# The first MLP's last 768 tokens by the seven-product 2x2 scheme that its second MLP already uses

## Chip, cores and metric

One core of one Trainium2 chip runs the kernel. The metric is device time in microseconds (us), the median of several executions; lower is better. TensorE (PE) multiplies, VectorE (DVE), ScalarE (ACT) and GpSimd (POOL) work element by element, SyncE (SP) issues nearly all DMA transfers.

## The reference

Attention over a window of 64 tokens on q, k, v of 4 x 8 x 576 x 64 gives `x`, 2304 tokens of 512 channels. Then come two MLPs, with the matrices `w_in` 512x2048, `w_out` 2048x512 in the first and `w_gate`, `w_val` 512x1536, `w_out` 1536x512 in the second:

```
h = x @ w_in
g = np.maximum(h, 0.0) + np.log1p(np.exp(-np.abs(h)))
x = g @ w_out
gate = 1.0 / (1.0 + np.exp(-(x @ w_gate)))
val = x @ w_val
return (gate * val @ w_out)
```

## The kernel before

Each float32 operand is kept as two fp32r tiles, a high part and the remainder, and each product is three matmuls into one accumulator (`mm3`, lines 393 to 396: high x high, high x low, low x high). All three lines appear with the same counts in the trace.

The first MLP goes block by block over the tokens (`BLOCKS1`, 512, 384, 384, 512 and 512). For each of 16 feature chunks f of 128, `m1_proj` (line 415) makes 12 matmuls into a bank `h0` or `h1`, ACT takes softplus in the bank (`m1_act`, 421) and writes the high part (`g_hi`, 426), DVE the low one (`g_lo`, 433), and two chunks later `m1_out` (438) makes 12 matmuls into four accumulator banks `acc0` to `acc3`. At a block's end `m1_copy` (450) drains them through a ring of three `stage` tiles (`STB`), and `m1_send` (458) stores them to the DRAM tensor `x2d`. The attention is done in 36 groups of 64 tokens: eight ahead of the first block, the others scattered between the blocks' matmuls. Groups of blocks 0 and 1 turn their probabilities on PE (`att_transpose`, 333), later ones with DVE and a trip through DRAM (`att_blocks`, `att_send`, `att_fetch`).

The second MLP (`m2_prod` 500, `m2_after` 532, `m2_out` 557) already uses a 2x2 block scheme: 768 tokens are two halves of 384, a quad is one 2x2 block of `w_gate` and `w_val`, and seven products M0 to M6 of combined weights and combined inputs stand for eight. The combined weights of a quad, 1.79 MB, are made during the first MLP (`c_sums` 193, `c_sum4` 204, `c_hi`, `c_lo`), stored to DRAM by `c_send`, and loaded by `wc_load` (237) through the two-buffer ring `xt`, which the first MLP's inputs use before. The inputs come back from `x2d` by `x2_load`, are combined by `x2_sum` and split by `x2_hi` and `x2_lo` (468 to 489).

The order of every engine's work is written into the program. Up to the first `m2_prod`, `lead_in` (944) places the operations of all engines by a model of their costs (`traits`, 786) and due times, keeping PE's sequence of `slots`; from there on the order is that of slots and offsets as written. Engines run their own queue in order and wait for each other by semaphores.

Of the kernel before, what the change touches and what calls it, by code (L numbers as in the profile page):

```python
# [41 lines left out]
def tile_kernel(ctx: ExitStack, tc: tile.TileContext, qk, vt, w1, w2, wg, wv, wo, out):  # L42
# [70 lines left out]
    place = list(range(NSLOT)) + [None] * len(seq2) + list(range(NSLOT - NF2, NSLOT))  # L113
# [77 lines left out]
    sum_t, send_t = {}, {}  # L191

    def c_sums(f):
        i = len(seq1) + 2 * f
# [6 lines left out]
        sum_t[f] = x  # L201

    def c_sum4(f):
        g = bits_t[len(seq1) + 2 * f].bitcast(F32)[:, 0]
        nc.vector.tensor_tensor(out=g[:, HC:], in0=g[:, HC:], in1=sum_t[f][:, HC:], op=ALU.subtract)

    def c_part(f, part):
        i = len(seq1) + 2 * f
        b = bits_t[i].bitcast(F32)
        if part in "av":  # L210
            k = "av".index(part)
            o = raw_t[i][:, k].bitcast(F32R).rearrange("p (e n) -> p e n", e=2)
            return b[:, k], o, 2 * k * DM
        if f not in send_t:
            send_t[f] = main.tile([P, 2, 2 * DM], U32, tag="raw", name="sumr", bufs=RB).bitcast(F32R)
        o = send_t[f]
        if part == "x":
            return sum_t[f], o[:, 0].rearrange("p (e n) -> p e n", e=2), 4 * DM
# [858 lines left out]
```

## Time and profile before

| | us |
|---|---|
| median of 3 runs (range) | 894.87 (894.35 to 895.14) |
| the profiled execution | 894.63 |
| its span in the trace | 892.8 |
| PE busy in the span | 884.1 (99%) |
| DVE, ACT, POOL busy | 523.7, 399.6, 153.7 |
| DMA queues busy, mean of 16 engines | 55.9% of the span, 177.59 MB |

The span runs from the first to the last instruction; the execution takes 1.8 us more around it. A matmul's row shows its own latency; because they are pipelined, the distance between starts is what one costs. The granted clock of PE is shown as a share of full speed.

### The profile page before, as it was taken

How to read it: one execution, taken by the hardware profiler on the slowest of the kernel's cores; microseconds unless marked ns; L12 is line 12 of the kernel's file. 1: busy time of each engine (PE TensorE's matmuls, PEld its weight loads, DVE VectorE, ACT ScalarE, POOL GpSimd, SP SyncE). 2: the span in 40 equal slices, each digit the busy share in tenths (PEclk: the TensorE clock that was granted, in tenths of full speed). 3: DMA queues.
4: the chain of work that ended last, by engine and by line, in shares of the span. 5: the costliest groups of instructions: out<-in, count | busy, mean ns of one | idle time of the engine just before them, and what ended most of it. 6: DMA issues, size and time to landing. Idle time of an engine off the chain costs nothing.

```text
span 892.8 us, 13509 instructions
## 1 busy us (share of the span) xinstructions
PE 884.1 (99%) x5033; PEld 796.5 (89%) x5035; DVE 523.7 (59%) x921; ACT 399.6 (45%) x892; POOL 153.7 (17%) x157
## 2 busy tenths in 40 slices
PE   9999999999999999999999999999999999999998
PEld 7688789999999888888889999999999999999997
DVE  5898876556555656365515667668445447444444
ACT  6867857546764755345323333334222225222222
POOL 4001102102110220002001333331111112111110
PEclk9999999999999999999999999999999999999999
DMA  9946346766786775683306565545454445544441
GB/s 348 395 158 207 134 163 211 248 198 229 265 270 208 239 235 163 212 284 130 130 1 255 221 256 201 206 176 216 178 212 156 161 163 208 185 165 165 165 166 72
DMA packets 56211, 177.59 MB, mean 199 GB/s; under 512 B 6096, under 2 KB 21456, under 8 KB 51536
## 3 DMA queue, kind: packets, MB, share of 16 engines
q1 hardware_dynamic: 56000, 176.58, 55.9%
q8 instruction: 40, 0.66, 0.3%
q14 instruction: 27, 0.22, 0.1%
q10 hardware_dynamic: 144, 0.13, 0.0%
HBM read 139.72 MB, written 36.96 MB: 198 GB/s over the span
## 4 chain that ended last, share of the span: by engine, by line
PE 98%; ACT 1%; DVE 1%; POOL 0%; issue 0%; POOLq 0%
PE h L394 17%; PE h L396 17%; PE h L395 17%; PE acc L394 11%; PE acc L395 11%; PE acc L396 11%; PE at L289 3%; PE at L376 2%; PE at L396 2%; PE at L395 2%; PE at L394 2%; PE acc L289 1%; PE h L406 1%; PE acc L338 0%; ACT w L179 0%; POOL w L330 0%
## 5 line engine op out<-in xcount | busy, mean ns | idle before, releaser
L512 DVE TENSOR_TENSOR w<-h,w 128x384 f32<-128x384 f32 x216 | 117.1, 556 | 159.5 <-PE h L396 156.8
L394 PE MATMUL h<-w,wc 128*128 128x384 f32 x504 | 169.0, 335 | 0.1
L396 PE MATMUL h<-w,wc 128*128 128x384 f32 x504 | 168.9, 335 | 0.0
L395 PE MATMUL h<-w,wc 128*128 128x384 f32 x504 | 168.7, 335 | 0.0
L524 POOL TENSOR_TENSOR g<-w,g 128x384 fp32r<-128x384 f32 x70 | 73.9, 1056 | 296.7 <-ACT g L517 252.1
L394 PE MATMUL h<-xt,w 128*128 128x512 f32 (+1 forms) x320 | 119.4, 373 | 0.6 <-ACT w L179 0.5
L394 PE MATMUL acc<-g,w 128*128 128x512 f32 (+1 forms) x320 | 119.5, 374 | 0.0
L396 PE MATMUL h<-xt,w 128*128 128x512 f32 (+1 forms) x320 | 117.9, 368 | 1.0 <-DVE w L187 1.0
L396 PE MATMUL acc<-g,w 128*128 128x512 f32 (+1 forms) x320 | 117.7, 368 | 0.0
L395 PE MATMUL acc<-g,w 128*128 128x512 f32 (+1 forms) x320 | 117.6, 368 | 0.0
L395 PE MATMUL h<-xt,w 128*128 128x512 f32 (+1 forms) x320 | 117.6, 368 | 0.0
L436 DVE TENSOR_TENSOR g<-h,g 128x512 fp32r<-128x512 f32 (+1 forms) x80 | 50.7, 634 | 82.9 <-ACT g L430 82.6
L394 PEld LDWEIGHTS h<-w,wc 128*128 128x128 f32 x504 | 94.6, 188 | 2.3 <-DVE w L512 0.4
L395 PEld LDWEIGHTS h<-w,wc 128*128 128x128 f32 x504 | 94.6, 188 | 2.0
L396 PEld LDWEIGHTS h<-w,wc 128*128 128x128 f32 x504 | 94.6, 188 | 0.0
L423 ACT ACTIVATE h<-h 128x512 f32<-128x512 f32 (+1 forms) x80 | 43.2, 540 | 106.6 <-PE h L396 104.4
L517 ACT CAST g<-w 128x384 fp32r<-128x384 f32 x72 | 36.9, 513 | 118.5 <-DVE w L512 118.5
L396 PEld LDWEIGHTS h<-xt,w 128*128 128x128 f32 x320 | 60.0, 188 | 9.5 <-DVE w L187 2.0
L394 PEld LDWEIGHTS h<-xt,w 128*128 128x128 f32 x320 | 60.1, 188 | 9.0 <-ACT w L179 0.6
L394 PEld LDWEIGHTS acc<-g,w 128*128 128x128 f32 x320 | 60.1, 188 | 8.0
L396 PEld LDWEIGHTS acc<-g,w 128*128 128x128 f32 x320 | 60.1, 188 | 7.7
L330 POOL TENSOR_TENSOR p<-p,st 128x512 f32<-128x512 f32 (+1 forms) x28 | 27.8, 996 | 226.8 <-DVE st L325 151.4
(129 smaller groups left out, 1438.5 us busy)
## 6 DMA issues: line engine op xcount, KB each, us to landing
wc<-wcd SPq DMA_DIRECT2D x36, 1792.0 KB, 7.2
qk<-in_qk SPq DMA_DIRECT2D x28, 512.0 KB, 4.8
wcd<-raw SPq DMA_DIRECT2D x24, 512.0 KB, 3.3
w<-in_w SPq DMA_DIRECT2D x16, 512.0 KB, 9.4
raw<-in_w SPq DMA_DIRECT2D x16, 512.0 KB, 4.6
v<-in_vt SPq DMA_DIRECT2D x25, 256.0 KB, 3.7
raw<-in_wg SPq DMA_DIRECT2D x12, 512.0 KB, 4.7
raw<-in_wv SPq DMA_DIRECT2D x12, 512.0 KB, 6.1
```

Source lines behind the costliest of these rows:

```text
L289: nc.tensor.matmul(out=s[:, j, :w], lhsT=t[:, 0, j, :], rhs=t[:, 1, j, :w], start=g >= NG0, stop=g >= NG0 or j == NPAIR - 1)
L330: nc.gpsimd.tensor_tensor(out=p[:, :, :w], in0=p[:, :, :w], in1=st[:, 2, :].unsqueeze(2).to_broadcast([P, NPAIR, w]), op=ALU.mult)
L376: nc.tensor.matmul(out=o[h * Q:(h + 1) * Q, j, :], lhsT=v[:w, (2 * j + h) * Q:(2 * j + h + 1) * Q], rhs=pt[:w, h, j], start=True, stop=True)
L394: nc.tensor.matmul(out=o, lhsT=lh, rhs=rh, start=first, stop=False)
L395: nc.tensor.matmul(out=o, lhsT=lh, rhs=rl, start=False, stop=False)
L396: nc.tensor.matmul(out=o, lhsT=ll, rhs=rh, start=False, stop=last)
L406: nc.tensor.matmul(out=idle["out"], lhsT=t[:, 0, :P], rhs=t[:, 1], start=True, stop=True)
L423: nc.scalar.activation(out=t, in_=t, func=AF.Softplus)
L436: nc.vector.tensor_tensor(out=g[:, 1, :n], in0=t, in1=g[:, 0, :n].bitcast(F32), op=ALU.subtract)
L512: nc.vector.tensor_tensor(out=out, in0=a, in1=b, op=op)
L517: nc.scalar.copy(out=g[:, 0, :HALF], in_=t)
L524: eng.tensor_tensor(out=g[:, 1, :HALF], in0=t, in1=g[:, 0, :HALF].bitcast(F32), op=ALU.subtract)
```

## The change

The first MLP's last 768 tokens leave the block loop; three blocks of 512 remain (`BLOCKS1`). The 768 tokens become one pass of eight quads (`NS1` = 1): a quad is a 2x2 block of `w_in`, two chunks of 128 features each way. Seven products of six matmuls of 384 columns (`s_prod`) are combined by ACT and DVE (`s_copy`, `s_mix`) into four feature-by-token parts; each gets softplus, high and low part (`s_act`, `s_hi`, `s_lo`), and then `s_out` multiplies three chunks of 128 tokens of each part with the features' 128 `w_out` rows, 512 wide, as the moving operand, into six accumulators laid token by channel. At the end `s_drain` turns each accumulator in 32x32 squares on DVE and `s_send` stores it to `x2d` by four DMAs in pieces of 32 floats.

The combined weights of these quads are rebuilt from the split weights in SBUF (`c_join` adds high and low) and take the same way through DRAM; those of the second MLP follow later (`COMBO1`, `COMBO2`: start and distance in us). The attention output of these 12 groups goes to DRAM (`att_out`, `att_put`, tensor `x1d`) and comes back by `x2_load`. The four first feature chunks of block 1 are done in two halves of 256 tokens (`SPLIT`). Attention is placed by times (`NEXT`, `REST`), all of it before the new stage. The planner now covers the new stage too, some of its constants change, and temporary tiles of the second MLP lie in other slots, five halves in place of six. In the second MLP's first quad PE's order is M0 M1 o0 o1 M2 M3 o2 M4 M5 o3 o4 M6 o5, as before, o0 to o5 being the last six `s_out`. The core of the diff:

```
-BLOCKS1 = [512, 384, 384, 512, 512]
+BLOCKS1, NS1, SPLIT = [512, 512, 512], 1, 4
...
+DENSE, NEXT, REST = (6.9, 11.0, 9.6), (62.8, 97.8), (120.5, 273.9)
+COMBO1, COMBO2, WOF, WOG, XT = (143.2, 12.7), (248.7, 17.4), 9.0, 12.0, 33.9
+URGE, FAR_MARGIN, X_MARGIN, HURRY = 10, 0.8, 2.0, 1.5
...
+    x1d = dram.tile([KC, P, NT - NT1], F32, tag="x1d", name="x1d")
     x2d = dram.tile([KC, P, NT], F32, tag="x2d", name="x2d")
-    wcd = [dram.tile([P, 14 * HC], F32, tag=f"wcd{f}", name=f"wcd{f}") for f in range(NF2)]
+    wcd = [dram.tile([P, 14 * HC], F32, tag=f"wcd{q}", name=f"wcd{q}") for q in range(NQ)]
...
+    def c_join(q, k):
+        if q not in join_t:
+            join_t[q] = main.tile([P, 2, DM], U32, tag="bits", name="bits", bufs=1)
+        w = w_t["w1", 2 * q + k].bitcast(F32)
+        nc.vector.tensor_tensor(out=c_bits(q)[:, k], in0=w[:, 0], in1=w[:, 1], op=ALU.add)
...
+    UNITS = []
+    for b, n in enumerate(BLOCKS1):
+        if b == 1 and SPLIT:
+            UNITS += [(b, 0, n // 2, 0, SPLIT), (b, n // 2, n, 0, SPLIT), (b, 0, n, SPLIT, NF1)]
+        else:
+            UNITS.append((b, 0, n, 0, NF1))
...
+    def att_out(g, engine):
+        x = main.tile([P, 512], F32, tag="stage", name="xo", bufs=STB)[:, :NPAIR * Q]
+        x_t[g] = x.rearrange("p (j n) -> p j n", j=NPAIR)
+        (nc.scalar.copy if engine == "act" else nc.vector.tensor_copy)(out=x_t[g], in_=o_t.pop(g))
+
+    def att_put(g):
+        t0 = g * Q - NT1
+        nc.sync.dma_start(out=x1d[:, :, t0:t0 + Q].rearrange("k p n -> p k n"), in_=x_t.pop(g))
+
+
     def mm3(o, lh, ll, rh, rl, first, last):
...
     def m1_proj(b, f):
-        n = BLOCKS1[b]
-        h = psum(f"h{f % 2}")[:, :n]
-        proj(h, w_t["w1", f], xt_t[b], n)
+        block, cols, n = cols_of(b)
+        h = psum(bank1[b, f])[:, :n]
+        proj(h, w_t["w1", f], xt_t[block][:, :, :, cols], n)
...
     def m1_out(b, f):
-        n = BLOCKS1[b]
+        block, cols, n = cols_of(b)
...
-        if f == 0:
-            acc_t[b] = [psum(f"acc{c}")[:, :n] for c in range(KC)]
+        if block not in acc_t:
+            acc_t[block] = [psum(f"acc{c}")[:, :BLOCKS1[block]] for c in range(KC)]
         for c in range(KC):
-            mm3(acc_t[b][c], w[:, 0, c * P:(c + 1) * P], w[:, 1, c * P:(c + 1) * P], g[:, 0, :n], g[:, 1, :n],
-                f == 0, f == NF1 - 1)
...
+            mm3(acc_t[block][c][:, cols], w[:, 0, c * P:(c + 1) * P], w[:, 1, c * P:(c + 1) * P], g[:, 0, :n], g[:, 1, :n],
+                f == 0 and not cols.start, f == NF1 - 1)
...
-        t0 = (2 * s + col) * HALF
-        nc.sync.dma_start(out=t, in_=x2d[2 * row:2 * row + 2, :, t0:t0 + HALF].rearrange("k p n -> p k n"))
+        src, t0 = (x1d, (2 * s + col) * HALF) if s < NS1 else (x2d, (2 * (s - NS1) + col) * HALF)
+        nc.sync.dma_start(out=t, in_=src[2 * row:2 * row + 2, :, t0:t0 + HALF].rearrange("k p n -> p k n"))
...
     def x2_hi(s, k, kc):
-        c = pair(2 * k, 1 + s, F32R, 2, DM)[:, kc, :, :HALF]
+        slot = index["w1", 2 * k + kc + 2]
+        c = pair(slot, 0, F32R, 2, DM)[:, slot % 2, :, :HALF]
...
+    AFTER = (2, 4, 5, 6)
+
+    def quad(j):
+        return half(0, (4, 3, 2, 4)[j])
+
+    def s_prod(s, f, k):
+        o = h_t[s, f, k] = psum(f"h{(7 * (s * NQ1 + f) + k) % 2}")[:, :HALF]
+        product(o, s, f, k)
+
+    def s_copy(s, f):
+        nc.scalar.copy(out=half(0, 0), in_=h_t.pop((s, f, 0)))
+
+    def s_mix(s, f, k):
+        m1, u2, lo, hi, sa = (half(0, i) for i in range(5))
+        o = h_t.pop((s, f, k))
+        if k == 1:
+            tt(u2, o, m1, ALU.add)
+        elif k == 2:
+            tt(sa, o, m1, ALU.add)
+        elif k == 3:
+            tt(lo, o, u2, ALU.add)
+        elif k == 4:
+            tt(hi, o, lo, ALU.add)
+            tt(u2, o, u2, ALU.add)
+        elif k == 5:
+            tt(lo, lo, o, ALU.subtract)
+        else:
+            tt(sa, o, u2, ALU.add)
+
+    def s_act(s, f, j):
+        nc.scalar.activation(out=quad(j), in_=quad(j), func=AF.Softplus)
+
+    def s_hi(s, f, j):
+        g = g_t[s, f, j] = main.tile([P, 2, NMAX], F32R, tag="g", name="g1", bufs=GB)
+        nc.scalar.copy(out=g[:, 0, :HALF], in_=quad(j))
+
+    def s_lo(s, f, j, engine):
+        g = g_t[s, f, j]
+        eng = nc.gpsimd if engine == "pool" else nc.vector
+        eng.tensor_tensor(out=g[:, 1, :HALF], in0=quad(j), in1=g[:, 0, :HALF].bitcast(F32), op=ALU.subtract)
+
+    def token_acc(s, c):
+        if (s, c) not in acc_t:
+            acc_t[s, c] = psum(f"acc{c}") if c < KC else psum("at", 2)
+        return acc_t[s, c]
+
+    def s_out(s, f, j, c):
+        g, w = g_t[s, f, j], w_t["w2", 2 * f + j % 3 % 2 + (j == 2)]
+        cols = slice(c * P % HALF, c * P % HALF + P)
+        mm3(token_acc(s, c), g[:, 0, cols], g[:, 1, cols], w[:, 0, :], w[:, 1, :], f == 0 and j < 2,
+            f == NQ1 - 1 and j > 1)
+
+    def s_drain(s, c):
+        x = x_t[s, "y", c] = main.tile([P, 512], F32, tag="stage", name="x2", bufs=STB)
+        nc.vector.transpose(out=x, in_=acc_t[s, c])
+
+    def s_send(s, c):
+        x, t0 = x_t.pop((s, "y", c)), NT1 + 2 * s * HALF + c * P
+        o = x2d[:, :, t0:t0 + P].rearrange("c (b x) n -> x (c b) n", x=32)
+        for a in range(4):
+            nc.sync.dma_start(out=o[:, :, 32 * a:32 * (a + 1)],
...
+    for c in range(NS1 * NQ1):
+        s, f = divmod(c, NQ1)
+        prods = [(s_prod, s, f, k) for k in range(7)]
+        late_q = [(s_out, s, f, j, 3 * j + i) for j in range(2) for i in range(3)]
+        outs = tail
+        for entry in "M0 M1 o0 o1 o2 M2 M3 o3 o4 o5 M4 M5 a0 a1 a2 M6 a3 a4 a5".split():
+            kind, k = {"M": prods, "o": outs, "a": late_q}[entry[0]], int(entry[1])
+            if k < len(kind):
+                slots.append(kind[k])
+        tail = [(s_out, s, f, j, (0, 3)[j - 2] + i) for j in (2, 3) for i in range(3)]
...
+        elif fn is s_out and f == NQ1 - 1 and rest[0] > 1:
+            c = rest[1]
+            at(i + 1, -50, s_drain, b, c)
+            at(i + 1, -49, s_send, b, c)
...
+    n1 = BLOCKS1[1] // Q // 2
+    for p in range(n1):
+        for k in range(2):
+            attention(NG0 + 2 * p + k, NEXT[0] + p * (NEXT[1] - NEXT[0]) / max(n1 - 1, 1), False)
+    nf = (NT // Q - NG0) // 2 - n1
+    for p in range(nf):
+        for k in range(2):
+            attention(NG0 + 2 * (n1 + p) + k, REST[0] + p * (REST[1] - REST[0]) / (nf - 1), False)
...
+    timely(when[s0] - XT, -1, swap_pools, 0)
+    for k, name in enumerate(NAMES):
+        timely(when[s0] - XT, k, x2_load, 0, name)
```

A seam is named below by its two sides: the one into the new stage follows the last block, the one out of it leads into the second MLP.

## Rows read from the trace of the kernel before

**Rows 1.** The page's first part: span, and busy time of each engine.

```profile
span 892.8 us, 13509 instructions
PE 884.1 (99%) x5033; PEld 796.5 (89%) x5035; DVE 523.7 (59%) x921; ACT 399.6 (45%) x892; POOL 153.7 (17%) x157
```

**Rows 2.** Busy time by stretch: PE, PEld, DVE, ACT, POOL, PEclk, DMA share, GB/s.

```profile
30.00:129.00 99.00, 97.47 (x544) 80.00 (x545) 87.15 (x126) 71.28 (x130) 5.69 (x6) 1.00 0.58 206
129.00:470.00 341.00, 341.00 (x2049) 306.70 (x2048) 188.12 (x340) 185.35 (x433) 46.34 (x43) 1.00 0.60 199
470.00:887.00 417.00, 416.93 (x2182) 388.62 (x2181) 229.12 (x411) 119.83 (x239) 90.10 (x83) 1.00 0.50 185
```

**Rows 3.** Timeline of PE, first block: first and last of 72 matmuls in a row.

```profile
60.19 0.39 PE L394 MATMUL h<-xt,w 128*128 128x512 f32 x1
...
76.28 0.39 PE L396 MATMUL acc<-g,w 128*128 128x512 f32 x1
```

**Rows 4.** Timeline of PE, second MLP: first and last of 21 matmuls in a row.

```profile
483.04 0.33 PE L394 MATMUL h<-w,wc 128*128 128x384 f32 x1
...
486.51 0.34 PE L396 MATMUL h<-w,wc 128*128 128x384 f32 x1
```

**Rows 5.** Groups by line and shape: count, busy us, mean ns, idle before.

```profile
L394 PE MATMUL h<-xt,w 128*128 128x512 f32 x192 | 75.9, 395 | 0.6 <-ACT w L179 0.5
...
L394 PEld LDWEIGHTS h<-xt,w 128*128 128x128 f32 x320 | 60.1, 188 | 9.0 <-ACT w L179 0.6 <-issue 0.6
...
L394 PE MATMUL h<-xt,w 128*128 128x384 f32 x128 | 43.5, 340 | 0.0
```

**Rows 6.** Timeline of PE around one attention group's transposes: start, duration in us.

```profile
108.30 0.60 PE L338 MATMUL at<-ident,p 128*128 128x128 f32 x4
108.66 0.48 PE L394 MATMUL h<-xt,w 128*128 128x512 f32 x1
108.97 0.40 PE L395 MATMUL h<-xt,w 128*128 128x512 f32 x1
```

**Rows 7.** Timeline of PE, first block, the longest hole after the start.

```profile
92.87 0.40 PE L395 MATMUL h<-xt,w 128*128 128x512 f32 x1
94.23 0.50 PE L396 MATMUL h<-xt,w 128*128 128x512 f32 x1 [0.96 <-DVE w L187]
```

**Rows 8.** Timeline of ACT: the exponentials of two attention groups, from table to table.

```profile
147.61 1.28 ACT L316 ACT_TABLE_LOAD   x1
...
153.71 0.47 ACT L423 ACTIVATE h<-h 128x384 f32<-128x384 f32 x1
```

**Rows 9.** Busy time by stretch, twenty us of the first block, columns as in Rows 2.

```profile
40.00:60.00 20.00, 20.00 (x90) 16.55 (x89) 19.03 (x27) 11.76 (x16) 0.00 (x0) 1.00 0.60 206
```

**Rows 10.** Groups by line and shape, columns as in Rows 5: DVE, POOL and ACT.

```profile
L512 DVE TENSOR_TENSOR w<-h,w 128x384 f32<-128x384 f32 x216 | 117.1, 556 | 159.5 <-PE h L396 156.8 <-issue 1.3 <-ACT w L533 1.2
...
L524 POOL TENSOR_TENSOR g<-w,g 128x384 fp32r<-128x384 f32 x70 | 73.9, 1056 | 296.7 <-ACT g L517 252.1 <-issue 42.8 <-PE h L396 1.9
...
L423 ACT ACTIVATE h<-h 128x384 f32<-128x384 f32 x32 | 15.2, 475 | 36.0 <-PE h L396 33.9 <-DVE bits L168 2.0
...
L228 POOL TENSOR_TENSOR raw<-bits,raw 128x512 fp32r<-128x512 f32 x7 | 9.1, 1295 | 57.2 <-ACT raw L223 57.2
```

**Rows 11.** DMA issues: count, KB each, median us from issue to landing.

```profile
wc<-wcd SPq DMA_DIRECT2D x36, 1792.0 KB, 7.2
...
pt<-pd SPq DMA_DIRECT2D x84, 64.0 KB, 3.1
...
x2d<-x SPq DMA_DIRECT2D x12, 256.0 KB, 2.1
```

**Rows 12.** Timeline at the seam into the second MLP: ACT, then PE.

```profile
479.01 0.59 ACT L454 COPY x<-acc 128x512 f32<-128x512 f32 x1 [1.60 <-DMA x2d<-x]
...
481.99 0.34 PE L396 MATMUL h<-w,wc 128*128 128x384 f32 x1
482.40 0.44 PE L394 MATMUL h<-w,wc 128*128 128x384 f32 x1
```

More of the change, by code (lines that the diff above doesn't have):

```diff
@@ L75, in tile_kernel @@
     NS2 = NT // (2 * HALF)
+    NSL = NS1 + NS2 - 1
+    NT1 = sum(BLOCKS1)
+    NQ1 = NF1 // 2
+    NQ = NQ1 + NF2
     NCH = 2 * HALF // P
@@ L112, in tile_kernel @@
     WO_AT = len(seq1) + len(seq2)
[L113 removed]
+    index = {key: i for i, (key, _) in enumerate(allw)}
+    place = list(range(NSLOT)) + [None] * len(seq2) + [index["w2", f] for f in range(NF2)]
     pair_t, raw_t, bits_t, w_t = {}, {}, {}, {}
@@ L200, in c_sums @@
         nc.vector.tensor_tensor(out=a21, in0=a11, in1=a21, op=ALU.subtract)
[L201 to L218, printed above, removed]
-        return b[:, 0, HC:], o[:, 1, :DM].rearrange("p (e n) -> p e n", e=2), 6 * DM
@@ new lines, in c_sum4, with c_part @@
+    def c_sum4(q):
+        g = c_bits(q)[:, 0]
+        nc.vector.tensor_tensor(out=g[:, HC:], in0=g[:, HC:], in1=sum_t[q][:, HC:], op=ALU.subtract)
+    def c_part(q, part):
+        if q < NQ1 and part == "a":
+            w = w_t["w1", 2 * q]
+            return None, w.rearrange("p e n -> p (e n)"), 0
+        if part == "s4":
+            if q not in send_t:
+                send_t[q] = main.tile([P, 512], F32R, tag="stage", name="sumr", bufs=STB)
+            return c_bits(q)[:, 0, HC:], send_t[q], 6 * DM
+        i = len(seq1) + 2 * (q - NQ1) if q >= NQ1 else ("c", q)
+        if i not in raw_t:
+            raw_t[i] = main.tile([P, 2, 2 * DM], U32, tag="raw", name="raw", bufs=RB)
+        k = int(part == "v")
+        t = sum_t[q] if part == "x" else c_bits(q)[:, k]
+        return t, raw_t[i][:, k].bitcast(F32R), "avx".index(part) * 2 * DM
@@ new lines, in tile_kernel, with attention, put @@
+    timed = {}
+    def attention(g, t, near):
+        odd = g % 2
+        if near:
+            def put(off, order, fn, *args):
+                at(t + off, order, fn, *args)
+        else:
+            def put(off, order, fn, *args):
+                timed[fn, *args] = t + 2.9 * off + order / 400
+        far = grp_block[g][0] >= FAR
+        put(0, 20, att_scores, g)
+        put(1, -30, att_max, g)
+        put(2, -30, att_exp, g)
+        put(4 - near, -33, att_sum, g)
+        put(4 - near, -32, att_norm, g)
@@ new lines, in traits @@
+        if fn is s_hi:
+            f, j = rest
+            return "act", 0.42, [(s_act, a, f, j)], [("g", GB, (s_out, a, f, j, 2 if j % 2 == 0 else 5))]
+        if fn is s_lo:
+            return THIRDS, 0, [(s_hi, a, *rest)], []
+        if fn is s_out:
+            f, j, c = rest
+            deps = [(s_lo, a, f, j), (*slots[pos[fn, a, *rest] - 1], None)]
+            if f == 0 and j < 2 and a == 0:
+                deps += [(m1_copy, NB1 - 1, k) for k in range(KC)] + [(att_out, g) for g in grp_block if g * Q >= NT1]
+            elif f == 0 and j < 2:
+                deps += [(s_drain, a - 1, c)]
+            return "pe", 0.68, deps, []
```

448 lines of the change are left out of this document (271 added, 177 removed).

## The prediction, made before the change was run

> **What bounds the kernel now.** I read the page's first part, then busy time by stretch, then the timeline of PE. PE is busy for 884.1 of 892.8 us [rows 1]. By stretch, PE is never idle from 129 to 470 us, and for 0.07 us from 470 to 887 [rows 2]; the first block's 99 us hold 1.53 us of idle time, most of it one hole in which PE waited for the low part of a weight: 1.36 us between starts where 0.23 is normal [rows 7]. So the time is the sum of what PE has to stream, at a granted clock of 1.00 (2.4 GHz). DVE is busy for 88% of the first block and 55% of the stretch to 470 us [rows 2]. Even at 19.03 of 20 us DVE held nothing up [rows 9]: a busy neighbour costs nothing here until one of its results comes late.
>
> **What one matmul costs.** From the first to the last of 72 matmuls of 512 columns are 71 distances in 16.09 us, 0.2266 us each [rows 3]; at 384 columns 20 distances take 3.47 us, 0.1735 us each [rows 4]. The line through both gives 0.1204 us at 256 columns.
>
> **PE, removed and added.** Rows 5 show one of six such lines each: the first MLP has 6 x 192 = 1152 matmuls of 512 columns and 6 x 128 = 768 of 384, so 261.0 + 133.2 = 394.3 us. Afterwards: blocks 0 and 2 have 768 matmuls of 512; block 1 has 12 x 24 = 288 of 512 and, in its split chunks, 2 x 4 x 24 = 192 of 256; the eight quads have 8 x 7 x 6 = 336 of 384 and 8 x 12 x 3 = 288 of 512. That is 1344 x 0.2266 + 336 x 0.1735 + 192 x 0.1204 = 304.6 + 58.3 + 23.1 = 386.0 us. The gain is **8.3 us**, small because only the projection loses a product in eight (48 matmuls, 8.3 us). The output products keep their columns; 512 in place of 384 wide saves 1.3 us of fixed cost and the split gives that back.
>
> The 256-column price is not in the trace. Its bounds are 0.107 (the columns alone at 2.4 GHz) and 0.1735 (the 384 row): -2.6 to +10.2 us over 192. A weight load lasts 188 ns [rows 5], but 384 columns already pass every 173 ns, so loads overlap; I take the line. The Trainium skill ("TensorE: Matmul & The Clock Gate", section "LDWEIGHTS (loading the stationary operand)") gives columns / 1.2 ns, 107 ns for 128. By that the load just fits under 120 ns; were the 188 ns row the pace, the sum would be 13 us worse. No run here shows 256 columns.
>
> **Attention on PE.** Eight groups in place of six turn on PE, since block 1 now has 512 tokens. One group's four transposes take 0.36 us and the next matmul 0.08 us more [rows 6]: **+0.9 us** for two. Scores and values stay 28 groups after the opening.
>
> **The first block and the split.** The first block carries up to four pairs of groups where it had three, beside a DVE at 88% [rows 2]. Bounds: the present hole goes (-1.1 us) or two like it come (+2.3); I take 0, as DVE at 95% held nothing up [rows 9]. In the split a step of PE is 12 x 0.12 = 1.44 us. A bank is wanted again one projection and two outputs later, 4.3 us, of which softplus, high and low part need some 1.2 us (475 ns for ACT's step at 384 [rows 10], less at 256). A pair's exponentials keep ACT from softplus for 6.1 us [rows 8]. One pair (`REST`, 137.5 + 6 us) falls there: 0 to 3 us, I take **+0.8**.
>
> **The new stage.** A quad is 42 x 0.1735 + 36 x 0.2266 = 15.4 us of PE. DVE mixes seven times, 3.9 us at 0.556; four low parts take 0.556 each on DVE or 1.056 on POOL [rows 10]. The eight extra weight sets cost DVE some 5 us each (two joins, three sums, a difference and three low parts, these on POOL at up to 1.295 [rows 10]). From 129 to 470 us DVE rises from 188 to some 188 + 31 + 18 + 40 - 17 (the blocks' low parts) = 260 us, 78%. Slack: a product's bank is wanted 3.1 us later, after one product and three outputs; its mix needs 0.6. The tightest wait is the second feature part: from M4 to its first output PE has M5, three outputs and M6, 4.1 us, against two mixes, two ACT steps of 0.48 and POOL's 1.06, some 3.2 with hand-overs. Cover of about 1 us: 0 to 8 us lost, I take **+0.5**, since the second MLP runs the same way with still less slack between products without a hole [rows 2].
>
> **Moved work.** The second MLP's sets are made later; inputs are copied, stored, reloaded, combined and split ahead of the stage, and again for the second MLP during it. All of this is ACT, DVE, POOL and DMA work with tens of us of lead: nothing on PE. Cover gone, a late set would cost one 7.2 us load [rows 11]. DMA gains 8 x 2 x 1.79 MB beside 177.6 and some 3 MB for the inputs, a share of 60% growing to about 70% [rows 2]. SP gets about 90 more issues and loses eight; new waits on it (inputs stored before they are reloaded, combined weights before their load) stand ahead of loads that are due later. I cost them at nothing, up to 2 us.
>
> **The seam out of the new stage.** Six DVE drains replace nothing the block loop had there except four copies, now earlier. Counting from the second MLP's M0, outputs end at 2.8, 3.4, 6.2, 8.9, 9.6 and 11.3 us. Only three stage tiles exist, so drains 3 to 5 wait for stores 0 to 2, and DVE, in order, then holds back the mixing of M4 to M6 behind them, for which PE waits as soon as its two banks are full. Before, such a wait (1.60 us, on ACT) let PE lose 0.24 us [rows 12]. A store is 256 KB in pieces of 128 bytes, not in the trace. Bounds: 2.1 us, like the same bytes in long rows; 12.4 us, four times the 3.1 us of a 64 KB fetch in 512-byte pieces [rows 11]. I take 3.3, nearer to the same bytes, since consecutive issues overlap. One after another from 3.6 us, the third then ends at 13.5, 2.1 after its drain could start; less 1 us of slack of the banks: **+1.1 us**. Below nothing it cannot go.
>
> **Sum.** 894.6 - 8.3 + 0.9 + 0.8 + 0.5 + 1.1 = 889.6 us against the profiled execution (span 892.8 and 1.8 around it); the median shown is 0.24 higher: **889.8 us**.
>
> **Rivals.** *Late stores at the seam (slower).* With T us per store PE loses 3.6 + 3T - 11.4 - 1.0 us. At T = 5.0 the rest of the gain is gone, from 5.6 the kernel is slower by 0.2%, at the upper end, 12.4, the time is about 917. For it: short pieces, a load of 1.79 MB just ahead of them in the queue, in-order DVE. Against: the copies before lost 0.24 us in the same place. The Trainium skill ("DMA: Bandwidth & Descriptors", Specifications) wants 512 bytes or more per piece for full rate and says that below it the engine reads before it writes. That rule speaks for this rival; if each store took twice the 3.3 us, 11.0 us would be lost and the time 899.7. Chance 0.12.
>
> *The chain within a quad takes the gain.* If DVE, with weight sets in front of the mixes, misses the second part's deadline by 1 us in each quad, 8 us go: 897.3. Against: rows 9. Chance 0.13, half of it with only a part lost, near 894.
>
> *256 columns do not come faster than 384.* 10.2 us back: 900.0. Against: loads overlap. Chance 0.07.
>
> **How the numbers follow.** The forecast has 0.68, with its own range 886.5 to 893: no new stall gives 887.4, the bounds of the split, first block and stage the rest. A measurement tells about 0.2% (1.8 us) from no change, so faster means below 893.1 and slower above 896.7. The forecast's mass and a sliver of the chain make faster 0.68; the chain's other part and a mild seam (T near 5) make same 0.14; the rest is slower, 0.18. The range must hold 0.8: 886.5 to 897.5 takes in the forecast, the chain, and a mild seam.
>
> **What would show it.** Right: 336 matmuls of 384 columns and 192 of 256 at 0.12 us between starts, PE at 100% in the new stage, second MLP's M0 some 6 us earlier. Wrong: starts 0.17 us apart at 256; holes in each quad that end with DVE or POOL; DVE waiting for `x2d` stores after the stage, PE idle behind it; a hole at 140 to 160 us behind softplus. The prediction fails if PE's holes after 129 us sum to over 6 us.

## The result, and the profile after

The changed kernel takes 905.82 us (median of 4 runs, 903.69 to 906.67) where the kernel before takes 894.85 us: a ratio of 1.012, 95% interval 1.0107 to 1.0132. It is slower by 11 us where 889.8 us were forecast, outside the range. Its profiled execution took 906.34 us. First the page's first part, to be held against [rows 1].

```profile
span 904.6 us, 13843 instructions
...
PE 884.3 (98%) x4995; PEld 782.1 (86%) x4995; DVE 590.1 (65%) x1045; ACT 422.0 (47%) x947; POOL 171.5 (19%) x172
```

The span is 11.8 us longer, yet PE's busy time is the same to 0.2 us: the MLPs have 48 matmuls less, so PE waits more, or is busy at a slower pace. The stretches say where. Columns as in [rows 2].

```profile
133.00:175.00 42.00, 42.00 (x358) 38.83 (x356) 28.62 (x65) 31.72 (x90) 10.94 (x11) 1.00 0.84 284
175.00:262.00 87.00, 86.97 (x545) 72.61 (x539) 62.18 (x118) 55.12 (x140) 16.52 (x16) 1.00 0.88 306
262.00:272.00 10.00, 7.05 (x34) 5.63 (x35) 6.20 (x14) 6.85 (x16) 3.35 (x3) 0.66 0.91 275
272.00:347.00 75.00, 75.00 (x436) 62.04 (x434) 53.97 (x90) 46.65 (x104) 14.83 (x13) 1.00 0.84 286
347.00:476.00 129.00, 124.62 (x613) 110.22 (x612) 94.22 (x165) 61.76 (x118) 15.42 (x13) 1.00 0.77 273
476.00:899.00 423.00, 421.27 (x2198) 391.33 (x2196) 235.17 (x422) 120.39 (x245) 91.10 (x84) 1.00 0.52 185
```

Three things are to be seen. PE is full from 133 to 262 us and nearly full behind 476. It loses 3 us in the ten from 262 and 4.4 us in the new stage (129 us less 124.62). And the DMA share in all of the middle is 0.77 to 0.91, where it was 0.60 [rows 2]; DVE, with 94.22 of 129 us, is at 73% and less loaded than in the first block. What the share did to transfers stands in the page's list of DMA issues (count, KB each, median us from issue to landing; 209.05 MB in all, where it was 177.59); [rows 11] has the store of a block end at 2.1 us.

```profile
wc<-wcd SPq DMA_DIRECT2D x44, 1792.0 KB, 7.4
wcd<-raw SPq DMA_DIRECT2D x52, 512.0 KB, 5.7
...
x2d<-x SPq DMA_DIRECT2D x12, 256.0 KB, 5.9
...
x2d<-x SPq DMA_DIRECT2D x24, 64.0 KB, 2.5
```

A 256 KB store now lands after 5.9 us in the median. The 7.4 us of the large load of 1.79 MB, where it was 7.2, say little: most of the 44 belong to the second MLP, at a share of 0.52, and the eight issued between 239 and 447 us took 8.0 to 10.6 us. So large loads are later in the full stretch too. The 256 KB parts of the sets, which had gone out in the busy stretch before, hardly changed (5.7 against 5.5). The chain of waits around the first loss (start, duration, what) shows who pays.

```profile
259.09 6.16 DMA x2d<-x
...
265.27 0.59 ACT x L498
...
265.91 0.80 PE acc L441
```

A store of the end of block 1, issued at 259.09, lands 6.16 us later. Only then has ACT a free tile in the ring of three for the copy of a further accumulator, and only behind this copy may PE write that bank. Part of the delay lies ahead of the transfer: the copy that the store sends had ended at 255.80, and SP issued the store 3.3 us later, right behind a load of 512 KB:

```profile
258.43 0.57 SPq L309 DMA_DIRECT2D qk<-in_qk  x1
259.09 0.45 SPq L503 DMA_DIRECT2D x2d<-x  x1
```

On PE:

```profile
262.68 0.40 PE L443 MATMUL acc<-g,w 128*128 128x512 f32 x1
265.91 0.80 PE L441 MATMUL acc<-g,w 128*128 128x512 f32 x1 [2.83 <-ACT x L498]
266.50 0.63 PE L442 MATMUL acc<-g,w 128*128 128x512 f32 x1
266.93 0.63 PE L443 MATMUL acc<-g,w 128*128 128x512 f32 x1
```

From 262.68 to 265.91 is one distance of 3.23 us instead of 0.23. Behind it matmuls of 512 columns start 0.43 us apart, nearly twice the 0.2266 of [rows 3]: the granted clock from 266 to 271 us is 0.50, the lower level of 1.2 GHz. So one late store of 256 KB took 3.0 us directly and some 2.5 us more by the clock (5 us at half of it).

In the new stage the same wait stands once at a block end (2.0 us at 362) and then behind the stores of the weight sets. The largest of those, in the chain, on ACT and on PE:

```profile
426.06 6.84 DMA wcd<-raw
432.92 0.62 ACT L241 CAST raw<-sums 128x512 fp32r<-128x512 f32 x1 [5.53 <-DMA wcd<-raw]
437.06 0.44 PE L441 MATMUL h<-w,wc 128*128 128x384 f32 x1 [1.99 <-ACT w L566]
```

A part of a set, 512 KB, takes 6.84 us to land before its tile in the ring `raw` of two is free. ACT, in order, stands 5.53 us in front of the next piece of work on weight sets, with the softplus and copies of the quad behind it.

All distances between PE's matmuls together give an account of both spans, in us. A distance is compared with the prediction's price for its columns; what is over is put to attention (when scores, transposes or values stand in between), to a hole (over by more than 0.14 us, a half clock among them), or to the pace (the rest).

| | before | after | difference |
|---|---|---|---|
| ahead of the first matmul of the block loop | 30.1 | 30.4 | +0.3 |
| matmuls at the prediction's prices | 803.2 | 794.9 | -8.3 |
| attention in between | 45.3 | 48.7 | +3.5 |
| holes | 1.5 | 12.8 | +11.3 |
| rest of the pace | 7.9 | 11.5 | +3.6 |
| behind the last matmul | 4.8 | 6.2 | +1.4 |
| span | 892.8 | 904.6 | +11.8 |

The second row is a count at the prediction's prices, so its 8.3 us show that the counts are right; what the prices missed is in the row of the pace. Of the 12.8 us of holes 5.8 lie ahead of the new stage, 5.0 in it and 2.0 behind it, nearly all at the seam. Behind 129 us they are 11.8, and the prediction had named 6 as the sum at which it fails. The first product of the second MLP starts at 480.1 us; before it was 470.4.

### The profile page after: what moved, and what is told of

Its sections match the earlier page's. It is cut to its first block, busy times and chain, and to the rows that moved or that the text cites. A ratio compares the mean times of both kernels' runs of the same rounds, so it can differ in the third digit from the quotient of the medians.

```text
span 904.6 us, 13843 instructions
## 1 busy us (share of the span) xinstructions
PE 884.3 (98%) x4995; PEld 782.1 (86%) x4995; DVE 590.1 (65%) x1045; ACT 422.0 (47%) x947; POOL 171.5 (19%) x172
## 2 busy tenths in 40 slices
DMA packets 79476, 209.05 MB, mean 231 GB/s; under 512 B 25520, under 2 KB 39856, under 8 KB 73776
## 4 chain that ended last, share of the span: by engine, by line
PE 84%; DMA 10%; ACT 2%; DVE 2%; issue 1%; SPq 0%; DVEq 0%; ACTq 0%
PE h L441 15%; PE h L443 15%; PE h L442 15%; PE acc L441 9%; PE acc L443 9%; PE acc L442 9%; DMA wcd<-raw 4%; PE at L324 2%; PE at L443 2%; PE at L442 2%; PE at L441 2%; PE at L411 2%; DMA x2d<-x 2%; DMA raw<-in_w 1%; DMA w<-in_w 1%; DMA w<-in_vt 1%
## 5 line engine op out<-in xcount | busy, mean ns | idle before, releaser
L553 DVE TENSOR_TENSOR w<-h,w 128x384 f32<-128x384 f32 x264 | 142.5, 555 | 166.8 <-PE h L443 162.8
L441 PE MATMUL h<-w,wc 128*128 128x384 f32 x616 | 207.5, 337 | 4.0 <-ACT w L566 2.0
L443 PE MATMUL h<-w,wc 128*128 128x384 f32 x616 | 206.7, 336 | 0.0
L442 PE MATMUL h<-w,wc 128*128 128x384 f32 x616 | 206.4, 335 | 0.0
L441 PEld LDWEIGHTS h<-w,wc 128*128 128x128 f32 x616 | 115.7, 188 | 10.2 <-ACT w L566 2.9
L442 PEld LDWEIGHTS h<-w,wc 128*128 128x128 f32 x616 | 115.6, 188 | 3.3
L443 PEld LDWEIGHTS h<-w,wc 128*128 128x128 f32 x616 | 115.6, 188 | 0.0
L441 PE MATMUL acc<-g,w 128*128 128x512 f32 (+1 forms) x208 | 80.4, 387 | 3.0 <-ACT x L498 2.8
L441 PE MATMUL acc<-w,g 128*128 128x512 f32 x208 | 81.0, 390 | 1.8 <-ACT g L590 1.8
L443 PE MATMUL acc<-w,g 128*128 128x512 f32 x208 | 82.4, 396 | 0.0
L442 PE MATMUL acc<-w,g 128*128 128x512 f32 x208 | 82.0, 394 | 0.0
L441 PE MATMUL h<-xt,w 128*128 128x512 f32 (+1 forms) x208 | 80.1, 385 | 0.5 <-ACT w L188 0.4
L443 PE MATMUL acc<-g,w 128*128 128x512 f32 (+1 forms) x208 | 78.3, 376 | 0.7 <-DVE w L196 0.7
L442 PE MATMUL acc<-g,w 128*128 128x512 f32 (+1 forms) x208 | 78.1, 376 | 0.0
L443 PE MATMUL h<-xt,w 128*128 128x512 f32 (+1 forms) x208 | 77.8, 374 | 0.0
L442 PE MATMUL h<-xt,w 128*128 128x512 f32 (+1 forms) x208 | 77.7, 373 | 0.0
L660 ACT ACTIVATE w<-w 128x384 f32<-128x384 f32 x36 | 18.9, 524 | 97.7 <-DVE w L553 97.5
L553 DVE TENSOR_TENSOR w<-w 128x384 f32<-128x384 f32 x72 | 40.1, 558 | 25.1 <-ACT w L660 21.5
L441 PEld LDWEIGHTS acc<-g,w 128*128 128x128 f32 x208 | 39.5, 190 | 11.0 <-ACT x L498 3.3
```

Source lines behind the costliest of these rows:

```text
L441: nc.tensor.matmul(out=o, lhsT=lh, rhs=rh, start=first, stop=False)
L442: nc.tensor.matmul(out=o, lhsT=lh, rhs=rl, start=False, stop=False)
L443: nc.tensor.matmul(out=o, lhsT=ll, rhs=rh, start=False, stop=last)
L553: nc.vector.tensor_tensor(out=out, in0=a, in1=b, op=op)
L660: nc.scalar.activation(out=sb, in_=u2, func=AF.Sigmoid)
```

## The experiments

Four theories. **A**: queues 77% to 91% busy land short stores late, and rings of two or three tiles hand that to PE. **B**: SP issues stores too late, in a bad order. **C**: the added work of DVE and ACT. **D**: the ring of stage tiles got too many users (block ends, attention outputs, the weights' fourth part).

**e1, thin stores.** All sets but the first keep their instructions, but store 32 floats a row, and all loads read the first set.

```
-        nc.sync.dma_start(out=wcd[q][:, at0:at0 + o.shape[-1]], in_=o.bitcast(F32))
+        n = o.shape[-1] if q == 0 else 32
+        nc.sync.dma_start(out=wcd[q][:, at0:at0 + n], in_=o.bitcast(F32)[:, :n])
...
-        nc.sync.dma_start(out=t.bitcast(F32), in_=wcd[f + NQ1 * (s >= NS1)])
+        nc.sync.dma_start(out=t.bitcast(F32), in_=wcd[0])
```

> Every engine's order and SP's issues stay; the stores of the combined weights of all quads but the first carry 32 floats a row in place of 1024 or 512, and every load of combined weights reads the first quad's (so the products use wrong weights; the load's bytes stay). It takes some 34 MB of stores off the stretch from 143 to 476 us. Theory A (the DMA queues, 84 to 91% busy there, land the short stores late that tiles of two small rings wait for): share of the queues at 175 to 262 us from 0.88 to about 0.6, landing of the block stores x2d<-x from 5.9 to about 2.5 us, holes of PE at 262, 362 and 434 us gone, 894 to 896. Theory B (SP's order: the store is issued late behind other waiting issues): issues and waits are the same, so the holes at 262 and 362 stay, 903 to 906. Theory C (DVE and ACT have too much work in the new stage): nothing changes, 904 to 906.

Measured: 895.55 us (894.31 to 896.49), ratio to the kernel before 1.0006 (0.9995 to 1.0018). In the middle stretches of e1:

```profile
133.00:175.00 42.00, 42.00 (x353) 38.84 (x353) 28.76 (x66) 31.73 (x90) 10.46 (x10) 1.00 0.60 196
175.00:262.00 87.00, 87.00 (x555) 73.03 (x551) 63.62 (x122) 56.66 (x146) 17.80 (x18) 1.00 0.66 203
262.00:347.00 85.00, 84.80 (x497) 70.23 (x496) 62.74 (x104) 53.64 (x114) 17.08 (x15) 1.00 0.61 196
347.00:476.00 129.00, 129.00 (x644) 116.39 (x644) 98.44 (x172) 66.27 (x125) 17.84 (x15) 1.00 0.54 189
```

With the share at 0.54 to 0.66 (last column but one) PE is full, with DVE and ACT as busy as before. 10.3 of the 11 us are a matter of transfers, not of C. How they came back is only in part as A has it. The block ends' stores land after

```profile
x2d<-x SPq DMA_DIRECT2D x12, 256.0 KB, 3.6
```

where 2.5 were expected, and at the end of block 1 the first of them still took 6.14 us (5.3 to 5.8 the others). But SP issued it 1.8 us behind the block's last matmul in place of 5.4, so the hole of 3.0 us shrank to 0.4. At the end of block 2 the first three fell from about 6 to about 3.5 us. So B, as recorded with unchanged issue times, isn't excluded here: lighter traffic also let SP issue sooner. And the kernel is only level with the one before, so transfers explain the loss and not the missing gain.

**e2, stores first.** The planner gives block-end stores the priority that copies have.

```
-            if key[0] in (s_copy, s_mix, s_act, s_hi, s_lo, m1_copy):
+            if key[0] in (s_copy, s_mix, s_act, s_hi, s_lo, m1_copy, m1_send):
```

> The planner gives the block stores the same 10 us of priority as the copies before them, so SP issues them earlier (3.3 us after its copy at the second block's end now). Theory B: the holes at 262 and 362 us vanish, about 898. Theory A: the landing still takes some 6 us, the hole at 262 shrinks by 3 at the most, 902 to 905. Theory C: no change.

903.29 us (900.19 to 907.52), ratio 1.0094 (1.0067 to 1.012). In its profiled execution (906.97 us) the hole at 262 splits into two of 1.3 and 0.6 us, the others stay or move; stores still land in 5.4 us. But the edit didn't do there what it was meant to: SP issues the first store at 260.11 us, 3.4 us after its copy and again right behind the 512 KB load. So this run doesn't decide on B; e10 comes back to it.

**e3, no copies of the attention output.** `att_out` and `att_put` do nothing, and the new stage loads other tokens from `x2d`.

```
-        src, t0 = (x1d, (2 * s + col) * HALF) if s < NS1 else (x2d, (2 * (s - NS1) + col) * HALF)
+        src, t0 = (x2d, (2 * s + col) * HALF) if s < NS1 else (x2d, (2 * (s - NS1) + col) * HALF)
```

> The attention output of the last 12 groups is neither copied nor stored, and the new stage loads tokens of the first blocks instead: 12 users of the three-tile ring less, and 12 stores of 256-byte pieces, 1.6 MB. Theory D (the ring is shared by too many users: block copies, attention copies, the weights' last part): the hole at 262 us goes or falls under 1 us, 898 to 900. Theory A: the ring still waits for a block store of some 6 us, a hole of 2 to 3 us stays, 902 to 905.

902.2 us (900.04 to 902.93), ratio 1.0075 (1.0048 to 1.0103). With these 12 users of the ring gone the hole at 262 shrinks from 3.0 to 0.8 us, though its store still takes 5.3 us (profiled execution: 900.04), but the new stage keeps 4.1 us of holes, at a share of 0.86 to 0.89. D has a part, and only at block ends.

**e4, a plain seam.** The seam's store becomes one DMA in rows of 512 bytes, which exchanges the 32x32 squares.

```
-        for a in range(4):
-            nc.sync.dma_start(out=o[:, :, 32 * a:32 * (a + 1)],
-                              in_=x[32 * a:32 * (a + 1)].rearrange("x (k t) -> x k t", t=32))
+        nc.sync.dma_start(out=x2d[:, :, t0:t0 + P].rearrange("c p n -> p c n"), in_=x.rearrange("p (c n) -> p c n", c=KC))
```

> The six drains after the new stage are stored by one DMA each in rows of 512 bytes (the 128 channels and 128 tokens of each square come out exchanged) in place of four DMAs in pieces of 128 bytes. If the short pieces make the seam's holes at 493 (1.1 us) and 504 us (0.7 us, a load of weights issued late), both go: 903.5 to 904.5. If the wait is for DVE's own order, the first stays: 905 to 906.

902.95 us (902.36 to 903.54), ratio 1.0087 (1.0058 to 1.0116). The holes behind the new stage fall from 2.0 to 0.5 us; those at 262 and 362 us stay (2.1 and 2.6 us). The seam thus gives 1.5 of the 2.9 us; two executions can't tell more.

**e5, the kernel before with a fuller queue.** In `att_send` of each far group:

```
+        for k in range(2):
+            extra = dram.tile([P, 2 * DM], U32, tag=f"extra{g}_{k}", name=f"extra{g}_{k}")
+            nc.sync.dma_start(out=extra, in_=allw[(2 * g + k) % 32][1])
```

> The kernel before, with nothing of the change but a fuller queue: each of the 22 far attention groups also copies 2 x 512 KB from DRAM to DRAM, with no reader, behind its own store (some 23 MB between 150 and 374 us, where the queue's share was 0.66 to 0.71). Theory A (a full queue lands the block ends' stores late, and the ring of three tiles passes that on to PE): share above 0.85, the 192 KB stores of block ends land in 5 us or more instead of 3.6, holes of 1 to 3 us at the block ends in this stretch, 897 to 901 us. Rival E (a full queue alone harms nothing: it needs the tighter plan of the changed kernel, with more users of the ring and sets made beside the new stage): late landings, but no hole over 0.5 us, 894 to 896 us. A hole in ordinary attention work (fetches late) would be a third case and would show as PE waiting for pt or v.

920.7 us (917.84 to 923.47), ratio 1.0286 (1.0267 to 1.0306): far worse than A had it, and through the third case. One thing differs from the recorded text: the edit puts the copies ahead of the group's own store, so that this store, `pd`, always stands right behind 1 MB. The landings that answer are these.

```profile
pd<-pd SPq DMA_DIRECT2D x20, 256.0 KB, 6.0
...
x2d<-x SPq DMA_DIRECT2D x8, 192.0 KB, 4.2
```

The share is 0.86 to 0.88 from 150 to 385 us. The 256 KB store of turned probabilities (`pd`, through one tile) takes 6.0 instead of 2.9 us, those of block ends 4.2 where 5 or more were expected, and in the profiled execution (917.84 us) the waits beside attention grow by 10 us (45.3 to 55.2, by the account above); holes grow by 10 more, a half clock among them. In the chain of waits from 150 to 400 us `pd` holds 20.7%, where before no DMA stood in it. The longest hole, 3.05 us at 419 us, is at a block end, but behind no block-end store: ACT's copy stands there behind the scaling of a weight whose load took 5.8 us and was itself held up on SP by a store of 9.6 us. So it isn't the block ends' stores alone: here a short transfer with little lead was hit in the attention too. What a share of 0.87 does without copies right ahead of `pd`, this run does not show.

**e6, thin stores and plain seam**, the edits of e1 and e4 together.

> The changed kernel with both reliefs together: combined weights stored in 32 floats a row (all but the first set, so the products of the other quads are of the first quad's weights), and the seam's store as one DMA in rows of 512 bytes (squares exchanged). If the thin stores removed 10.3 us and the plain seam removes what is left there, 893.3 to 894.3 us: the change's own gain with neither DMA loss, only 1 to 1.5 us better than before, not the 8.3 us of fewer matmuls; then a further 4 to 5 us of the forecast went to terms that are no stall of a transfer. If the two reliefs were the same waits counted twice, 895.5 us as with thin stores alone. If the rest were seam and second MLP only, under 892 us.

892.95 us (892.35 to 894.1), ratio 0.9978 (0.9969 to 0.9987), 0.35 below the range expected. Without either loss the change is worth 2.0 us. Its account has holes of 1.7 us, near the 1.5 of before; attention with 47.1 and pace with 10.8 us keep 1.9 and 3.0 of the 8.3, the two ends of the span 1.7 (the end behind the last matmul is 4.3 to 6.2 us from run to run). A part of the pace is the output of the new stage, its nine matmuls of 512 columns in a row here in the timeline of PE after (the first, the last, and the one behind):

```profile
380.05 0.39 PE L441 MATMUL acc<-w,g 128*128 128x512 f32 x1
...
381.90 0.39 PE L443 MATMUL at<-w,g 128*128 128x512 f32 x1
382.13 0.33 PE L441 MATMUL h<-w,wc 128*128 128x384 f32 x1
```

2.08 us for nine are 0.231 each, not 0.2266; over 288 that makes 1.3 us. Attention's extra is 0.9 at the forecast's price of the two groups' transposes, and 1.0 that has no single place.

**Can the waits be planned away, with the whole traffic kept?** e7 puts the fourth copy of a block end and the seam's drains 3 to 5 into tiles that lie idle then, and gives the planner other times (the sets' stand here, others of the kind changed with them); e8 keeps the ring of three at block ends, with its own times; e9 has the seam's tiles alone.

```
-        x = main.tile([P, 512], F32, tag="stage", name="x2", bufs=STB)
+        tag, bufs = ("stage", STB) if c < STB else ("sums", 1)
+        x = main.tile([P, 512], F32, tag=tag, name="x2", bufs=bufs)
...
-        x = x_t[s, "y", c] = main.tile([P, 512], F32, tag="stage", name="x2", bufs=STB)
+        if c < STB:
+            x = main.tile([P, 512], F32, tag="stage", name="x2", bufs=STB)
+        elif c == STB:
+            x = main.tile([P, 512], F32, tag="sums", name="x2s", bufs=1)
+        else:
+            if (s, "y") not in x_t:
+                x_t[s, "y"] = main.tile([P, 4, 512], F32, tag="raw", name="x2r", bufs=RB)
+            x = x_t[s, "y"][:, c - STB]
+        x_t[s, "y", c] = x
...
-COMBO1, COMBO2, WOF, WOG, XT = (143.2, 12.7), (248.7, 17.4), 9.0, 12.0, 33.9
+COMBO1, COMBO2, WOF, WOG, XT = (136.63, 12.32), (258.73, 18.18), 9.0, 12.0, 30.08
```

> The changed kernel, whole computation and whole traffic, with the waits on late stores designed away: the fourth copy of a block end goes into the tile of the weights' sums instead of the ring of three; at the seam drain 3 takes that tile and drains 4 and 5 a tile of the raw ring; and the planner gets other times (weight sets 12.3 and 18.2 us apart from 136.6 and 258.7, slower DMA, 2.2 us of margin on landings, attention 3 us later). If theory A holds in its sharp form (the loss is not the traffic, but short stores that something waits for), the queue stays at 0.8 or more from 133 to 476 us and stores still land in 4 us or more, yet holes over 0.5 us behind the first block are gone, second MLP's first product at 468.5 to 471 us instead of 480.1, 893 to 896 us in all. If the traffic as such must cost PE time (any plan runs into it, as the kernel before did with copies added), holes come elsewhere (attention, weight loads) and it stays over 900 us.

902.97 us (902.37 to 903.93), ratio 1.0084 (1.007 to 1.0098). The holes up to the seam are gone, at a share of 0.74 to 0.88, but for one of 1.7 us at the end of block 1, where stores again stand behind the 512 KB load and take 6.1 to 8.1 us; at the end of block 2 they take 2.0 to 2.1. The second MLP's first product starts at 468.2 us, 11.9 us sooner. Then 13.2 us are lost in its first quad.

```profile
469.27 0.34 PE L441 MATMUL h<-w,wc 128*128 128x384 f32 x1
472.92 0.45 PE L442 MATMUL h<-w,wc 128*128 128x384 f32 x1 [3.32 <-DVE w L533]
...
473.43 0.52 PE L441 MATMUL h<-w,wc 128*128 128x384 f32 x1
473.75 0.52 PE L442 MATMUL h<-w,wc 128*128 128x384 f32 x1
```

PE waits for `x2_lo` (L533), the low parts of the second MLP's inputs, which stand on DVE behind the last weight set; a half clock follows. This wait has nothing to do with a transfer: a plan that I had changed only for the queue let the last set begin at 458.7 us.

> As the run above, but block ends keep the ring of three for all four copies (seam tiles and other planner times, found for this ring: sets 14.5 and 17.1 us apart from 144.0 and 257.0). If the plan's times carry most of the gain, 894 to 898 us; if the ring is what counts at the block ends, holes of 1 to 3 us stay at 262 and 360 us, and it lands at 898 to 903 us.

899.27 us (898.52 to 899.89), ratio 1.0043 (1.003 to 1.0057). The ring of three alone makes no hole at the block ends here (0.2 us ahead of the new stage in all); other times carry it. 1.8 us are lost in the new stage and 6.2 behind the seam.

> The changed kernel with only the seam's drains 3 to 5 in other tiles, plan and ring otherwise unchanged, stores in their 128-byte pieces. Prediction's seam term: 1.1 us, drains waiting for stores 0 to 2. If right in kind, the holes at 493 and 504 us go (1.5 to 2 us together), 903.5 to 904.5 us. If the short pieces themselves are the cost (the load of weights queued behind them lands late), the hole at 504 stays and less than 1 us is gained.

906.13 us (903.99 to 906.84), ratio 1.0116 (1.0103 to 1.013): a miss. The hole at 493 us is gone, that at 503 grows to 2.0 us with a half clock behind it. The drains were one wait; e12 takes up what stood behind it.

**e10 and e11, e7 with the last set early**, each with its own times. The recorded texts leave out that e10 also has the edit of e2, the priority of block-end stores, and e11 has not. In e10:

```
-COMBO1, COMBO2, WOF, WOG, XT = (136.63, 12.32), (258.73, 18.18), 9.0, 12.0, 30.08
+COMBO1, COMBO2, WOF, WOG, XT = (144.02, 10.79), (245.75, 17.44), 9.0, 12.0, 34.02
...
-            if key[0] in (s_copy, s_mix, s_act, s_hi, s_lo, m1_copy):
+            if key[0] in (s_copy, s_mix, s_act, s_hi, s_lo, m1_copy, m1_send):
```

> The run with the fourth copy and the seam's drains in other tiles, once more with its whole computation and traffic, but with planner times that finish the last weight set well before the second MLP's first product (sets 10.8 and 17.4 us apart from 144.0 and 245.8, so the last begins at 437.6 and not at 458.7 us). There the holes had moved to 469 and 476 us, where the second MLP's inputs waited behind that set on DVE: 13.2 us at and behind the seam. If that was the plan's fault alone, the first product of the second MLP starts at 468 to 471 us, holes behind the seam sum to under 2.5 us, 893.5 to 896.5 us in all, equal to the kernel before, with the queue still at 0.8 or more from 133 to 347 us. If the traffic only moves its cost from one place to the next, holes of 2 us and more come up at another place and it stays over 899 us.

892.08 us (890.91 to 894.1), ratio 0.9972 (0.9963 to 0.9982): faster than both kernels. Its stretches:

```profile
133.00:175.00 42.00, 42.00 (x322) 39.30 (x321) 32.47 (x71) 30.69 (x88) 8.71 (x9) 1.00 0.83 286
175.00:262.00 87.00, 87.00 (x553) 72.38 (x552) 61.47 (x117) 59.05 (x150) 20.08 (x20) 1.00 0.90 307
262.00:347.00 85.00, 85.00 (x497) 70.32 (x497) 59.38 (x102) 50.68 (x107) 14.63 (x13) 1.00 0.88 297
347.00:468.00 121.00, 120.83 (x603) 108.73 (x602) 96.36 (x171) 62.76 (x120) 10.10 (x9) 1.00 0.79 276
468.00:886.00 418.00, 415.60 (x2172) 386.52 (x2170) 232.58 (x418) 117.37 (x238) 88.73 (x82) 1.00 0.52 187
```

PE loses 0.2 us from 133 to 468 us at a share of 0.79 to 0.90, as full as in the slow kernel, with the same bytes. The queue's share is no cost by itself. It doesn't fix the landings either: here those of the block ends are

```profile
x2d<-x SPq DMA_DIRECT2D x12, 256.0 KB, 2.5
```

and the first three at the end of block 1 take 2.4 to 3.0 us, at a share of 0.98 from 252 to 256 us. They go out ahead of the load behind which the changed kernel's store stood:

```profile
252.21 1.31 SPq L504 DMA_DIRECT2D x2d<-x  x3
253.62 0.46 SPq L309 DMA_DIRECT2D qk<-in_qk  x1
```

The same shows in the other runs of the changed kernel. Where the first store of this block end stands right behind a load of 512 or 256 KB it takes 4.3 to 6.2 us (the changed kernel, e1 to e4, e6, e7, e9, e11), where it stands ahead of it 2.4 to 3.3 (e8, e10, e12). Apart from the two runs with thin stores the largest hole here is 0.8 to 3.0 us in the first kind, and there is none in the second. These plans differ in other times too, so this is order and landing seen together, not an experiment on order alone; but it is B at the place that A was read from.

> The same edits with a third set of planner times (sets 14.5 and 17.2 us apart from 136.1 and 247.7, attention's pairs up to 279 us, slower DMA in the model), to see how far the result hangs on one choice of times. Expected like its neighbour, 894 to 897 us, if the two tiles and an early last set are what counts; over 899 us if the neighbour's times were luck.

894.26 us (892.88 to 897.77), ratio 0.9994 (0.9983 to 1.0005). One hole of 1.45 us at a block end is left, with its stores behind a load. Neighbouring plans differ by 2 us; how much of that is the priority of the stores and how much the times, no run separates.

**e12, the load first.** In e10 the one hole left (1.6 us at 490) waits for a load of weights. The timeline of SP in e10 (a row covers several DMAs; us is from the first to the last):

```profile
470.70 6.83 SPq L625 DMA_DIRECT2D x2d<-x  x12
...
478.32 2.19 SPq L625 DMA_DIRECT2D x2d<-x2s  x4
480.61 2.92 SPq L625 DMA_DIRECT2D x2d<-x2r  x4
483.63 0.46 SPq L257 DMA_DIRECT2D wc<-wcd  x1
```

The four DMAs of store 4, in pieces of 128 bytes, hold SP for 2.92 us, ahead of the load.

```
-            at(i + 1, -49, s_send, b, c)
+            behind = c in (STB, STB + 1)
+            at(pos[m2_prod, NS1, 0, 6] + 1 if behind else i + 1, c - 47 if behind else -49, s_send, b, c)
```

> The fast run above with one thing moved on SP: stores 3 and 4 of the seam are issued behind, not ahead of, the load of the weight set for the second MLP's third quad. There SP spent 2.9 us on store 4 ahead of that load, which so was issued at 483.6 us, landed 7.9 us later, and PE waited 1.6 us for it at 489.9 us. If SP's order is the cause of this one hole, the load goes out 3 to 5 us sooner, the hole at 490 us is gone and the time is 890.2 to 891 us. If the load only waits for its buffer or the queue, the hole stays within 0.5 us and the time at 892 us.

890.29 us (889.54 to 892.18), ratio 0.9947 (0.9933 to 0.996). The load goes out 12.5 us behind the second MLP's first product instead of 16.9, and the hole is gone:

```profile
480.48 0.38 SPq L257 DMA_DIRECT2D wc<-wcd  x1
480.96 4.60 SPq L625 DMA_DIRECT2D x2d<-x2s  x4
```

So B holds here by an experiment of its own, and in e9 the same load, issued at 496.6 us behind the same stores, landed at 504.5, where the hole that grew ended. With nothing left out this kernel is 0.5% faster than the one before. Its account has 0.8 us of holes.

## Why the prediction was wrong

**PE's sum** held in its counts, and 256 columns are 0.12 us apart; the pace took 3.0 of the 8.3 us back (e6). The timeline of PE in the split, after:

```profile
133.65 0.28 PE L443 MATMUL h<-xt,w 128*128 128x256 f32 x1
133.77 0.28 PE L441 MATMUL h<-xt,w 128*128 128x256 f32 x1
...
134.13 0.28 PE L441 MATMUL h<-xt,w 128*128 128x256 f32 x1
```

The rival with 0.07 is out. The Trainium skill's rule of columns / 1.2 ns for a weight load ("TensorE: Matmul & The Clock Gate", "LDWEIGHTS (loading the stationary operand)") is not contradicted, 107 ns would fit under these 120, but the trace does not confirm it either: its rows of the weight loads here last 188 to 191 ns each, so the loads overlap. The new stage's output was priced at the block loop's pace, 1.3 us short, and attention 1.0 us short.

**Moved work** is the step that failed: "a share of 60% growing to about 70%", "I cost them at nothing, up to 2 us". It cost 10.3 us (e1). The bytes were right, the division wrong. Some 31 MB were set against the 177.6 MB of the whole kernel, but they all fall between 133 and 476 us, where the kernel before moved 68 MB (199 GB/s for 341 us [rows 2]). The stage's own share then comes to 0.60 x (68 + 31) / 68 = 0.87; the stretches after give 0.83 in the mean. And any share below 1 was read as free, while a short transfer that is issued behind others lands late. The same paragraph counted "about 90 more issues" on SP, whose waits "stand ahead of loads that are due later": at the end of block 1 they stood ahead of a store that was due at once. The trace of before had a sign of it, one line of the same list that I had not read: the 2.1 us of [rows 11] are a median over blocks 0, 3 and 4, in which four of the twelve stores took 3.9 to 4.7 us, and this line has blocks 1 and 2.

```profile
x2d<-x SPq DMA_DIRECT2D x8, 192.0 KB, 3.6
```

Fewer bytes, 3.6 instead of 2.1 us, at a share of some 0.7. "Tens of us of lead" was true of the loads of sets and inputs. It was not true of the stores, neither those of block ends nor those of the sets' parts in the new stage, for whose tile other work waits within the same 6 to 7 us.

**The split** (+0.8) and **the chain in a quad** (+0.5, the rival with 0.13): no hole in the split, and without late transfers (e6) none in the stage. The holes that were there end with ACT and DVE, but behind a store: the releaser in a row of PE is the last link only, and the chain of waits has the DMA further back.

**The seam** (+1.1): two holes of 1.1 and 0.7 us, the first where the prediction put it, drains behind stores; the third store ended 12.4 us behind the second MLP's M0, where 13.5 were forecast. What the short pieces themselves cost stays open, since e4 changes their length and the number of DMAs together. At the second hole a load stood behind these stores in SP's order, which the prediction had put at nothing under moved work (e12). The rival of late stores at the seam had the right mechanism at the smallest of its places; the same wait stood at the ends of blocks 1 and 2 and in the new stage, where the forecast had none.

That e12 lands within 0.5 us of the 889.8 forecast is luck in part: of its 4.0 us in the account the forecast's -8.3 stand, but attention costs 2.0, the pace 2.4 and the two ends 0.6, while the holes, which the forecast let grow by 2.4, shrink by 0.7.

What stays open: which of the planner's times in e10 carry the gain, and how much of it is the priority of the stores. They were changed together, and neighbours differ by 2 us. Open too is how much of each late store in the changed kernel is its late issue and how much its landing, outside the places shown.

## What to carry to other kernels

When traffic is added, set it against the bytes of the stretch in which it falls, not of the whole kernel, and where that comes near 0.9, list every short transfer that something waits for through a ring of few tiles, with what stands ahead of it in its queue. A share of 0.90 cost nothing in a plan with such stores early and ahead of the loads (e10), and 10 us and more in two where they stood behind (the changed kernel, e5). And check in the trace that a change of priority changed the order before reading its time (e2). Holes move: after each repair look for the next wait, and keep the work of the stage behind it in the plan.
